# A fused retention and MLP kernel: the first queries and keys split over two DMA queues, and two decays moved from ScalarE to GpSimd

## The chip, the cores and the metric

The kernel runs on one core of one Trainium2 chip. A core has a TensorE (matrix products), a VectorE (DVE in the profile), a ScalarE (ACT), a GpSimd (POOL) and a SyncE (SP, which here only issues transfers). They run side by side and wait for each other through semaphores. SyncE and ScalarE each issue transfers between device memory (DRAM) and on-chip memory (SBUF) on a queue of their own. Matrix products land in PSUM, which TensorE writes and VectorE and ScalarE read.

The metric is device time in microseconds of one execution; lower is better.

## What is computed

First a recurrent retention over 768 tokens, for 4 batches and 8 heads of size 64. Its output, laid out as 3072 tokens of 512 numbers, goes through a two-layer network with a leaky ReLU.

```python
for t in range(S):
    state = gamma[None, :, None, None] * state + np.einsum('bhd,bhe->bhde', k[:, :, t], v[:, :, t])
    y[:, :, t] = scale * np.einsum('bhd,bhde->bhe', q[:, :, t], state)
...
x = np.ascontiguousarray(attn_out.transpose(0, 2, 1, 3)).reshape(B * S, H * D)
h = x @ w_in          # 512 -> 2048
g = np.maximum(0.01 * h, h)
return (g @ w_out)    # 2048 -> 512
```

The weights come as 64-bit floats, and the chip makes 32-bit floats of them.

## The kernel before

**Tiling.** The 768 tokens of a batch are six chunks (c = 0 to 5) of 128. In a chunk the recurrence is written as products: scores of keys and queries, masked (`score`, `masked`), scores times values (`values`), and the state that is carried on (`first_state` for chunk 0). The decay gamma to the power of t is taken out of the products: the values v are multiplied beforehand by a factor for token and head (`decay_v`, L160), and the sums afterwards by another (`tokens_taken`, L300, whose line in the profile is L308). The network is cut into four units of 512 hidden columns; its products are combined in the manner of Strassen, seven for eight.

**Order.** The schedule is by hand: each engine's instructions run in the order of the code, and waits are put in by the framework from what each instruction reads and writes. Chunk 0, batches 0 to 3, is handled as the inputs arrive, and in between the first weight pieces are converted. All the work around the change lies in the first 26 us.

**Steps that the prediction speaks of**, in the order of TensorE:

- `keep_busy(10)` (L897): ten filler products on zeros.
- `score(0, 0)` (L193), on queries and keys of batch 0. `heads[c, b][0]` has shape 128 x 2 x 4 x 128: part 0 of the second axis is the queries, part 1 the keys. The keys are the stationary operand, the queries the moving one.
- three small products (L915 to L919) that spread the table of decays. ScalarE copies the result (L922), and `decay_v` waits for it.
- `score(0, 1)`, then L927, a product that spreads the query factors, which ScalarE copies at L931.
- `values(0, 0)` and `values(0, 1)` (L263 and L252), `score(0, 2)`.
- `direct(0, 0, x, ..., 0)` (L695): the first hidden products, in four steps. Step n needs weight piece n, converted.
- between its steps: `values(0, 2)`, `score(0, 3)`, the states of chunk 0 (L278) and `values(0, 3)`.

**Conversion of a weight piece.** ScalarE makes the powers of two from the top bits (`powers`: L591, L595, L596), VectorE the mantissas (`mantissas_begun`: L603 and L608; `mantissas_ended`: L615, which multiplies the two). L603, L608 and L615 read SBUF only.

**Decays of v.** `decay_v` has two forms. On GpSimd it is one multiplication of 128 x 512 by a broadcast factor (L163). On ScalarE it is eight activations of 128 x 64, one for each head (L167). In chunk 0, batches 0 and 1 take the first form and batches 2 and 3 the second.

**Transfers at the start.** SyncE issues, in this order: queries and keys of batch 0 (`load_qk`, L121), v of batches 0 and 1 (`load_v`, L124), weight pieces 0 and 1 (L542), queries and keys of batch 2, v of batch 2, pieces 2 and 3, queries and keys and v of batch 3, and the keys in their second layout (`load_k`, L127). ScalarE issues queries and keys of batch 1, and the table of decays (L868), which waits for memsets of GpSimd and VectorE (L866, L867). Each transfer counts up one of eight semaphores in turn, so the ninth waits until the first has landed.

Of the kernel before, what the change touches and what calls it, by code (L numbers as in the profile page):

```python
# [22 lines left out]
def kernel(  # L23
# [14 lines left out]
    nc = tc.nc  # L38
# [30 lines left out]
    def unit_tile(k, name):  # L69
        if k in LATE or k in (0, 2):  # L70
            return work.tile([128, 7, 2, 256], FP32, tag=f"late{k}", name=name)
        return const.tile([128, 7, 2, 256], FP32, name=name)
# [32 lines left out]
    heads = {}  # L105
# [14 lines left out]
    def load_qk(c, b, queue=nc.sync):  # L120
        queue.dma_start(out=heads[c, b][0], in_=qk[c, b])  # L121

    def load_v(c, b, queue=nc.sync):
        queue.dma_start(out=heads[c, b][1][:, 1], in_=kv[c, b][:, 1])  # L124
# [30 lines left out]
    def load(c, b, place=None):  # L155
        place_for(c, b, place)
        load_qk(c, b)
        nc.sync.dma_start(out=heads[c, b][1], in_=kv[c, b])

    def decay_v(c, b, engine=nc.gpsimd):  # L160
        v = vals[c, b] if c >= JOINED else heads[c, b][1][:, 1]
        if engine is not nc.scalar:
            engine.tensor_tensor(out=v, in0=v,  # L163
                                 in1=gk[c].unsqueeze(2).to_broadcast([128, H, D]), op=ALU.mult)
        else:
            for h in range(H):
                engine.activation(v[:, h], v[:, h], AF.Identity, scale=gk[c][:, h : h + 1])  # L167
# [43 lines left out]
    def masked(c, b):  # L211
        am = new_am(c, b)
        nc.vector.tensor_tensor(
            out=am.rearrange("p j m n t -> p j m (n t)"),
            in0=scores[c, b].rearrange("p j m n t -> p j m (n t)"),
            in1=mask.rearrange("p n t -> p (n t)").unsqueeze(1).unsqueeze(1)
                .to_broadcast([128, 2, HP // 2, 3 * C // 2]), op=ALU.mult)
        scores[c, b] = am
# [355 lines left out]
    def next_mantissas():  # L574
        begin_mantissas()
        end_mantissas()
# [283 lines left out]
    rows = t[:, 1:3].rearrange("p i k n -> p (i k n)")[:, 0 : decay.shape[1]]  # L860
    nothing = t[:, 0, 0, 0:64].bitcast(BF16)
    half = decay.shape[1] // 2
    load_qk(0, 0)
    load_qk(0, 1, nc.scalar)
    nc.vector.memset(t[:, 0, 0, 0:64], 0.0)
    nc.gpsimd.memset(rows[:, :half], 0.0)  # L866
    nc.vector.memset(rows[:, half:], 0.0)  # L867
    nc.scalar.dma_start(out=rows[0:H], in_=decay)  # L868
    load_v(0, 0)
    load_v(0, 1)  # L870
    load_piece(0)
# [13 lines left out]
    for s in range(2):  # L885
        part = mask[ts(s, 64), 0 : 3 - s : 2 - s]
# [22 lines left out]
    def scratch(name, n):  # L909
# [22 lines left out]
        out=dec[:, 0:n_gq], in_=spread.rearrange("p i n -> p (i n)")))  # L932
# [6 lines left out]
    steps = direct(0, 0, x, parts[0][1], 0)  # L939
    next(steps)  # L940
    next_mantissas()
    decay_v(0, 2, nc.scalar)
    load(1, 2, unit_tile(LATE[0], "in12"))
    masked(0, 2)
    next_powers()
# [4 lines left out]
    score(0, 3)  # L950
    taken(0, 2, x)
    masked(0, 3)
    decay_v(0, 3, nc.scalar)
    next(steps)
    sums0 = two_banks("sums0")
    for b in range(B):
# [532 lines left out]
    for n in range(N2):  # L1489
# [16 lines left out]
        part = gs.pop(n)  # L1506
# [167 lines left out]
```

## Time and profile before

| what | us |
|---|---|
| median of 3 runs (630.54 to 631.47) | 631.17 |
| the profiled execution | 631.22 |
| its span, first to last instruction | 629.3 |

| stretch of the span, us | TensorE busy | VectorE busy | ScalarE busy | GpSimd busy |
|---|---|---|---|---|
| 0 to 13 | 11.55 | 5.69 | 5.27 | 3.33 |
| 13 to 26 | 11.99 | 9.41 | 10.39 | 0.00 |
| 26 to 37 | 10.71 | 8.66 | 10.57 | 0.20 |
| 37 to 629 | 588.58 | 488.61 | 255.16 | 102.24 |

The first table gives the whole time and what the profile covers of it: the span runs from the first to the last instruction, and 1.9 us of the execution lie outside. The second table gives the busy time of four engines in four stretches. A busy time close to the stretch's length means that the engine has hardly a hole there. TensorE's granted clock is 1.00 in all of them.

In the lines of a timeline the first number is the start in us from the begin of the span, the second the duration, then engine, line of the code, operation, what it writes and reads, and at the end, in brackets, how long the engine was idle before it and which work ended that. Names of tiles: `kv` and `in` hold inputs, `ap` the scores, `yp` the sums over values, `d` the hidden products, `w` a weight unit, `raw` a piece of 64-bit weights, `dec` the decay factors.

### The profile page before, as it was taken

Reading aid. Unit: us, or ns where it says so; the run is one execution under the profiler, and the core shown is the slowest. Engines: PE = TensorE matmul, PEld = TensorE weight load, DVE = VectorE, ACT = ScalarE, POOL = GpSimd, SP = SyncE. Lnnn points to the kernel's source line nnn. Section 1 sums busy time; section 2 is a strip of 40 time slices with the busy share of each in tenths; the row PEclk is TensorE's granted clock in tenths of the full one; section 3 lists DMA queues with packets and bytes.
Section 4 is the critical chain, followed back from the end, with each engine's and each line's share of the span. In section 5 each row is a group of like instructions: output and inputs, shape, how many; then the busy total and the mean of one; then the engine's idle time right before and its main releaser. Section 6 shows DMA issues by size and latency. Waiting matters only on the chain.

```text
span 629.3 us, 15220 instructions
## 1 busy us (share of the span) xinstructions
PE 622.8 (99%) x6375; PEld 572.2 (91%) x6375; DVE 512.4 (81%) x793; ACT 281.4 (45%) x543; POOL 105.8 (17%) x109
## 2 busy tenths in 40 slices
PE   8999999999999999999999999999999999999997
PEld 5888888888888889899999999999999999999996
DVE  5679769889979986679888968789968689977796
ACT  5876646446444114352433433534514435534540
POOL 2000000000010110105133052331250321333030
PEclk9999999999999999999999999999999999999999
DMA  8941425547782998396976996988478568678601
GB/s 328 405 143 34 126 75 193 167 133 252 243 296 73 347 333 272 101 339 190 349 228 215 283 333 240 324 280 280 150 257 298 156 216 281 209 264 278 205 1 68
DMA packets 105939, 140.99 MB, mean 224 GB/s; under 512 B 4488, under 2 KB 84232, under 8 KB 105872
## 3 DMA queue, kind: packets, MB, share of 16 engines
q1 hardware_dynamic: 105568, 139.41, 66.6%
q8 instruction: 50, 0.82, 0.5%
q10 hardware_dynamic: 304, 0.62, 0.3%
q14 instruction: 17, 0.14, 0.1%
HBM read 113.54 MB, written 26.48 MB: 222 GB/s over the span
## 4 chain that ended last, share of the span: by engine, by line
PE 94%; DVE 2%; ACT 1%; DMA 1%; issue 0%; SPq 0%; DVEq 0%; ACTq 0%
PE bank L1390 27%; PE bank L1311 12%; PE bank L1351 10%; PE bank L674 9%; PE C_h L674 4%; PE B_o L674 4%; PE A_h L674 4%; PE A_o L674 4%; PE C_o L674 4%; PE B_h L674 4%; PE D_o L674 2%; PE D_h L674 2%; PE d L695 2%; DMA raw<-in_weights_dram 1%; PE bank L371 1%; PE bank L453 1%
## 5 line engine op out<-in xcount | busy, mean ns | idle before, releaser
L619 DVE TENSOR_TENSOR made<-made,bank 128x512 f32<-128x512 f32 (+1 forms) x96 | 55.9, 617 | 39.8 <-PE bank L1390 35.9
L1390 PEld LDWEIGHTS bank<-x,wb 128*128 128x128 f32 x672 | 77.4, 192 | 1.2 <-ACT bank L1394 0.2
L1390 PE MATMUL bank<-x,wb 128*128 128x128 f32 x672 | 78.4, 276 | 0.0
L622 DVE TENSOR_TENSOR g<-g 128x512 f32<-128x512 f32 x96 | 64.0, 688 | 5.2 <-ACT g L1432 0.5
L1390 PE MATMUL bank<-x,wa 128*128 128x128 f32 x512 | 67.7, 275 | 0.0
L1394 ACT COPY bank<-bank 128x512 f32<-128x512 f32 (+1 forms) x32 | 16.6, 517 | 104.6 <-PE bank L1390 97.4
L1390 PEld LDWEIGHTS bank<-x,wa 128*128 128x128 f32 x512 | 62.7, 192 | 0.5 <-ACT made L1400 0.2
L1390 PE MATMUL bank<-t,wa 128*128 128x128 f32 x384 | 53.4, 275 | 0.0
L619 DVE TENSOR_TENSOR g<-made 128x512 f32<-128x512 f32 x64 | 49.0, 786 | 2.9
L1351 PE MATMUL bank<-g,w 128*128 128x256 f32 x216 | 48.5, 381 | 0.0
L1390 PEld LDWEIGHTS bank<-t,wa 128*128 128x128 f32 x384 | 48.0, 192 | 0.0
L1311 PE MATMUL bank<-g,w 128*128 128x128 f32 x368 | 47.0, 276 | 0.0
L1351 PEld LDWEIGHTS bank<-g,w 128*128 128x128 f32 x216 | 40.3, 190 | 5.4
L1311 PEld LDWEIGHTS bank<-g,w 128*128 128x128 f32 x368 | 43.8, 192 | 0.0
L1432 ACT ACTIVATE g<-g 128x512 f32<-128x512 f32 x64 | 37.7, 633 | 6.9 <-DVE g L619 6.9
L1290 POOL TENSOR_TENSOR x<-g 128x512 f32<-128x512 f32 x12 | 16.6, 1382 | 138.2 <-DVE t L622 40.1
L674 PE MATMUL bank<-g,w 128*128 128x256 f32 x168 | 38.0, 382 | 0.0
L674 PEld LDWEIGHTS bank<-g,w 128*128 128x128 f32 x168 | 31.3, 190 | 4.2
L619 DVE TENSOR_TENSOR o<-o,bank 128x512 f32<-128x512 f32 (+2 forms) x44 | 26.5, 633 | 9.8 <-ACT bank L788 4.2
L619 DVE TENSOR_TENSOR o<-o,w 128x2048 f32<-128x2048 f32 (+2 forms) x17 | 28.9, 1722 | 0.2
L674 PE MATMUL A_h<-x,w 128*128 128x256 f32 x112 | 26.6, 380 | 0.0
L163 POOL TENSOR_TENSOR in<-in,dec 128x512 f32<-128x512 f32 x2 | 2.4, 1232 | 139.7 <-DMA in<-in_kv_dram 139.7
(257 smaller groups left out, 1261.1 us busy)
## 6 DMA issues: line engine op xcount, KB each, us to landing
wa<-kept SPq DMA_DIRECT2D x16, 1344.0 KB, 8.7
w<-leaf_kept SPq DMA_DIRECT2D x44, 448.0 KB, 5.4
raw<-in_weights_dram SPq DMA_DIRECT2D x31, 512.0 KB, 4.4
wb<-kept SPq DMA_DIRECT2D x16, 896.0 KB, 6.0
wa<-kept SPq DMA_DIRECT2D x16, 448.0 KB, 4.7
wb<-kept SPq DMA_DIRECT2D x16, 448.0 KB, 6.8
out_dram<-o SPq DMA_DIRECT2D x23, 256.0 KB, 2.9
kept<-w SPq DMA_DIRECT2D x12, 448.0 KB, 5.7
```

Of the source, the lines that this page charges most:

```text
L371: nc.tensor.matmul(at[j][ts(h, 64), n, m, i], lhsT=x[ts(j, 64), 1, a, ts(h, 64)], rhs=x[ts(j, 64), 0, a, ts(h, 64)], start=(n == 0 and a = ...
L453: mm = nc.tensor.matmul(at[n][j][ts(i, 64), m, ts(h, 64)], lhsT=val[ts(h, 64), 2 * a + j], rhs=weights[j][ts(h, 64), n, m, i], start=(n == ...
L619: return nc.vector.tensor_tensor(out=out, in0=a, in1=b, op=ALU.add)
L622: return nc.vector.tensor_tensor(out=out, in0=a, in1=b, op=ALU.subtract)
L674: nc.tensor.matmul(to, lhsT=block(w, sa)[:, k, ts(i, 128)], rhs=rhs[:, k, a:z], start=(first and (i == 0 or split) and n == 0 and k == 0), ...
L695: nc.tensor.matmul(banks[r][:, i, :], lhsT=block(2 * u, r + 2 * kh)[:, k, ts(i, 128)], rhs=x[:, 2 * kh + th, k, :], start=(step == 0 and i ...
L1290: op = nc.gpsimd.tensor_tensor(out=out, in0=a, in1=b, op=ALU.subtract)
L1311: nc.tensor.matmul(ps[q][:, to], lhsT=leaf_weights[i][j], rhs=moving[s][:, i], start=(i == 0 and m in ("M1", "M5", "M4")), stop=True, skip ...
L1351: nc.tensor.matmul(room[x][:, i, :], lhsT=block(2 * u + 1, sa)[:, k, ts(i, 128)], rhs=rhs[:, k, :], start=(first and i == 0 and k == 0), s ...
L1390: nc.tensor.matmul(ps[q][:, i], lhsT=w[:, j, i], rhs=part_of(moving[i], s), start=(i == 0 and m in ("M1", "M5", "M4")), stop=True, skip_gr ...
L1394: nc.scalar.copy(out=ps[3], in_=ps[0])
L1432: nc.scalar.activation(g[:, i], g[:, i], AF.Prelu, alpha=0.01)
```

## The change

The queries and keys of batches 0 and 1 are no longer loaded in one transfer of 512 KB for each batch, but in two of 256 KB. SyncE issues the queries of batch 0 and of batch 1, ScalarE the keys of batch 0, then the table of decays, then the keys of batch 1. The values of batches 2 and 3 of chunk 0 are multiplied on GpSimd (L163, one instruction for each batch) and no longer on ScalarE (L167, eight for each batch). The numbers that are computed are the same.

```diff
-    load_qk(0, 0)
-    load_qk(0, 1, nc.scalar)
+    def load_part(b, part, queue):
+        queue.dma_start(out=heads[0, b][0][:, part], in_=qk[0, b][:, part])
+
+    for b in range(2):
+        load_part(b, 0, nc.sync)
+    load_part(0, 1, nc.scalar)
     nc.vector.memset(t[:, 0, 0, 0:64], 0.0)
     nc.gpsimd.memset(rows[:, :half], 0.0)
     nc.vector.memset(rows[:, half:], 0.0)
     nc.scalar.dma_start(out=rows[0:H], in_=decay)
+    load_part(1, 1, nc.scalar)
     load_v(0, 0)
     load_v(0, 1)
...
-    decay_v(0, 2, nc.scalar)
+    decay_v(0, 2)
...
-    decay_v(0, 3, nc.scalar)
+    decay_v(0, 3)
```

## The prediction

> **What bounds the kernel now.** I read the page first.
>
> ```profile
> PE 622.8 (99%) x6375; PEld 572.2 (91%) x6375; DVE 512.4 (81%) x793; ACT 281.4 (45%) x543; POOL 105.8 (17%) x109
> ```
>
> TensorE is busy 622.8 of 629.3 us. A change at the start can therefore only move the moments at which TensorE works; what it is late by at 26 us it is late by at the end. The second view is the list of TensorE's waits, over the whole span: it shows all that an edit could win there.
>
> ```profile
> PE idle L897 <- DVE t L865: 1.1, 1, 1.1
> PE yp L252 <- issue: 0.7, 1, 0.7
> PE d L695 <- DVE w L615: 0.4, 1, 0.4
> PE ap L193 <- DMA qk<-in_qk_dram: 0.2, 1, 0.2
> PE bank L436 <- DVE made L619: 0.2, 1, 0.2
> ```
>
> The change touches the 0.2 (first scores wait for the first batch's data) and what leads to the 0.4 (first hidden products wait for a converted weight piece). Third, the timeline of TensorE and then of VectorE and GpSimd, from 0 to 20 us (start, duration, engine, line, operation, idle before and what ended it).
>
> ```profile
> 1.05 4.45 PE L897 MATMUL idle<-t 128*128 128x512 bf16 x10 [1.05 <-DVE t L865]
> 5.74 1.20 PE L193 MATMUL ap<-qk 64*64 64x128 f32 x32 [0.24 <-DMA qk<-in_qk_dram]
> 13.38 3.86 PE L695 MATMUL d<-x,w 128*128 128x256 f32 x16 [0.35 <-DVE w L615]
> ```
>
> ```profile
> 9.60 0.92 DVE L603 TENSOR_SCALAR w<-raw 128x512 uint32<-128x512 uint32 x1
> 10.84 0.69 DVE L308 TENSOR_TENSOR x<-yp,dec 128x512 f32<-128x512 f32 x1 [0.33 <-ACT z L595]
> 12.65 0.68 DVE L615 SCALAR_TENSOR_TENSOR w<-w,z 128x512 f32<-128x512 f32 x1
> 13.24 0.42 DVE L603 TENSOR_SCALAR w<-raw 128x512 uint32<-128x512 uint32 x1
> 13.70 0.69 DVE L608 SCALAR_TENSOR_TENSOR w<-raw,w 128x512 f32<-128x512 uint32 x1
> 14.50 0.69 DVE L615 SCALAR_TENSOR_TENSOR w<-w,z 128x512 f32<-128x512 f32 x1
> ```
>
> ```profile
> 8.19 2.04 POOL L163 TENSOR_TENSOR kv<-kv,dec 128x512 f32<-128x512 f32 x2 [5.76 <-ACT dec L922]
> ```
>
> What to see: the ten filler matmuls end at 1.05+4.45 = 5.50, so the scores' wait is 0.24 and no more. From 10.84 to 15.19 VectorE works without a hole: tokens of batches 0 and 1 (L308), then pieces 0 and 1 of the weights (L603, L608, L615). Its L615 of piece 0 ends at 13.33 and releases the first hidden step at 13.38; that of piece 1 ends at 15.19, just when step 0's half of the 3.86 us ends (13.38+1.93 = 15.31). VectorE has no slack there, and TensorE none to give. And L603 took 0.92 while GpSimd's decays ran (to 10.23), 0.42 when they didn't.
>
> Last, the transfers of v of batches 2 and 3, from views of the DMA issues in the windows 5.7 to 6.05 and 7.9 to 8.2 (KB, us to landing): issued at 5.72 and 7.95, they land at 12.3 and 17.9.
>
> ```profile
> in<-in_kv_dram SPq DMA_DIRECT2D x1, 256.0 KB, 6.6
> ```
>
> ```profile
> in<-in_kv_dram SPq DMA_DIRECT2D x1, 256.0 KB, 10.0
> ```
>
> **What the Trainium skill says.** SBUF — State Buffer, Who interferes with whom: a VectorE instruction with two SBUF inputs, or in a two-port mode, and a GpSimd one that reads SBUF exclude each other for the whole instruction; who comes first goes first; a VectorE instruction with one PSUM input is left alone. The trace agrees: the masks L213 (from PSUM) took 0.96 beside GpSimd, as without; at 182 to 185 us, where this same decay meets the same conversion, both engines stretch (timeline of VectorE, then GpSimd):
>
> ```profile
> 182.32 0.69 DVE L615 SCALAR_TENSOR_TENSOR last<-last,z 128x512 f32<-128x512 f32 x1
> 183.93 1.26 DVE L603 TENSOR_SCALAR last<-raw 128x512 uint32<-128x512 uint32 x1 [0.92 <-ACT z L595]
> ```
>
> ```profile
> 182.49 2.42 POOL L163 TENSOR_TENSOR in<-in,dec 128x512 f32<-128x512 f32 x2 [139.72 <-DMA in<-in_kv_dram]
> ```
>
> Two decays alone take 2.04, here 2.42: the first came during L615 and was let through at 183.01, some 0.9 before its end. DMA: Bandwidth & Descriptors, Issuing engines are not separate DMA queues: another issuer saves issue time, not transfer time. The trace agrees in that the two first loads of 512 KB, one on each queue, take 4.9 and 5.1 us to landing.
>
> **The change, part by part.**
>
> Queries and keys. The same 1 MB is cut into four loads of 256 KB. The first half of each of the two 512 KB loads now is all that the first scores need. Both queues move about 0.4 MB per us together (390 to 430 GB/s in most slices of the transfers' view); the whole landed at 5.7 to 5.9, so 512 KB fewer means some 1.3 us less: 4.4 to 4.6, an estimate. That is ahead of 5.50, where the fillers end: the gain is the wait, 0.24, not the 1.3. The keys of batch 1 are issued on ScalarE behind the table of decays (issued at 1.59, held by memsets), near 2.1, and still land about 6, since the bytes are the same; they are needed at 7.5. ScalarE's table load, moved from 2.15 to about 2.6, takes 1.28 and has until 7.6.
>
> SyncE. One more issue ahead of v and piece 0: 0.45. Also, at most eight transfers are in flight: in before the seventh issue of SyncE (ScalarE had two) stands until 5.72, for the first load. With two more loads, piece 1 (2.88 now) becomes the ninth and stands until the first queries have landed, about 4.5. Cost nothing: the queue is full of earlier bytes until piece 0 lands at 9.10. If that cover were gone, piece 1 would cost what it lands after 12.1 instead of 10.4. Rows of 2 KB in place of 4 KB: v's 256 KB take 0.68 us in the stream, half of a 512 KB piece 0.64; over 1 MB that is 0.15. So piece 0 lands at 9.25 to 9.3. ScalarE's L591 and copy L931 then end at 10.5 instead of 10.32, and L308 can start at 10.60 instead of 10.84 (its sums come 0.24 earlier). Slack 0.1; hence the 0.24 arrives whole.
>
> Eight ScalarE activations per batch go (2.00 us each at 13.32 and 19.04). ScalarE is freed, and piece 2 is ready for VectorE 0.5 us earlier (L603 at 16.59 had waited 0.53 for ScalarE). But TensorE runs through from 15.24 to 23.3 with no hole, so this wins nothing.
>
> Two GpSimd multiplies come in, 1.04 us each alone. The first can start when v of batch 2 is there: 12.33+0.12 = 12.45. VectorE by then, 0.24 earlier than now: L615 of piece 0 from 12.41 to 13.09, L603 13.0, L608, L615 of piece 1 to 14.95. All four take two SBUF inputs or the two-port mode. If L615 is first by its 0.04 us, GpSimd holds the ports from 13.09 for 0.9, to 13.99; L603 ends 0.28 after that (as at 10.23 to 10.51), at 14.27 instead of 13.42: +0.85, and L615 of piece 1 ends at 15.80. Step 1 of the hidden products starts at 15.84 instead of 15.24: +0.60. If GpSimd is first, L615 of piece 0 ends near 13.95, step 0 starts at 14.0 (+0.62) and all else moves with it. Both orders give +0.6. Below: if v came after 15 us, or the ports weren't held, -0.24.
>
> The second starts at 18.0, where VectorE does L615 of piece 2 (18.0 to 18.7, moved). TensorE needs that at 19.45 (18.85+0.6). Held back by GpSimd it would end at 19.6: 0 to 0.2 more; I take 0, as the slack is 0.75. L308 and the masks read PSUM and aren't held. The decayed v are needed at 17.8 and 22; GpSimd has them by 14 and 19.1.
>
> Sum: -0.24 + 0.85 = +0.6. From 26 us on the critical chain hangs on TensorE's steps (ScalarE's activations follow them), so it stays. Against the profiled execution, 631.22 (span 629.3 and 1.9 around it): 631.8. It is 0.05 over the median of the runs, so the median too comes to 631.8.
>
> **Rivals.**
>
> Gain only (21%): VectorE makes up for the hold, because GpSimd takes a free place or the ports aren't claimed. For: L603 already stood behind decays at 9.6 without harm. Against: no hole from 10.84 to 15.19. 631.2-0.24 = 630.9; with the 0.66 hole of TensorE at 23.3 (the trace calls it issue; not explained) closed, 630.3.
>
> Slower (19%): the second hold decides too. If VectorE comes to piece 2 more than 0.75 late (point of decision: L615 of piece 2 would end, unhindered, after 19.45), the second hold of 0.9 falls on TensorE as the first did: -0.24+0.85+0.9 = +1.5, 632.7. For: a decay of the pair at 205.5 took 1.49 in such a meeting. Against: the 0.5 us that ScalarE gives back.
>
> No earlier start (7%): the first keys or queries land only near 5.7, since the queues interleave in another way than by halves. Then +0.85: 632.0.
>
> **How the numbers follow.** Forecast 631.8 (53%; its own range 631.3 to 632.4). What a measurement of this kernel can tell from no change is 0.2%, 1.26 us: bounds 629.9 and 632.4. Slower than that: nearly all of the slower rival and a few hundredths of the others: 0.21. Faster: the far end of gain only, 0.04. Range 630.6 to 632.8: it takes in gain only down to part of the closed hole, and the slower rival's middle.
>
> **What would show it.** Scores L193 at 5.50 with no wait for DMA; L163 on GpSimd at about 12.5 or 13.1; one of L615 and L603 there at 1.2 us or more; a hole of 0.6 to 0.9 in TensorE before L695 at 13 to 16 us; no ScalarE L167 at 13 and 19. The prediction is wrong if L163 falls where VectorE reads PSUM or rests, if piece 0 lands after 9.4, or if TensorE's lateness at 26 us isn't what is found at the end.

## The result and the profile after

| kernel | median us | runs | ratio of the runs to before, 95% interval |
|---|---|---|---|
| before | 630.77 | 19 | 1 |
| changed | 632.23 | 19 | 1.0027 (1.0021 to 1.0033) |

The medians differ by 1.46 us; the ratio, which is made from means, says 0.27%, some 1.7 us. It is a slowdown that the measurement can tell. The time lies in the predicted range, 0.43 over the forecast of 631.8, and in part by luck: the forecast was +0.6 on a median of three runs, 631.17, which lies 0.4 above the median of the 19 runs of the kernel before here. The change costs more than twice the +0.6, about what the slower rival said (+1.5), and not for that rival's reason. The profiled execution took 631.97 us with a span of 630.0, only 0.7 more than the span before. That 0.7 looks like the forecast's +0.6 and is not the same thing; the chain of causes is another one, as the timelines show.

TensorE in the changed kernel (line numbers are 5 higher below the edit; start, duration, line, idle before):

```profile
5.43 1.38 PE L193 MATMUL ap<-qk 64*64 64x128 f32 x32
8.06 0.90 PE L193 MATMUL ap<-qk 64*64 64x128 f32 x32 [0.49 <-DMA qk<-in_qk_dram]
12.40 0.90 PE L193 MATMUL ap<-in 64*64 64x128 f32 x32 [0.37 <-DMA in<-in_qk_dram]
13.71 1.99 PE L695 MATMUL d<-x,w 128*128 128x256 f32 x8
16.42 1.99 PE L695 MATMUL d<-x,w 128*128 128x256 f32 x8 [0.71 <-DVE w L615]
20.02 1.99 PE L695 MATMUL d<-x,w 128*128 128x256 f32 x8
```

The first scores start right behind the fillers, 0.31 earlier than before. The second scores, at 7.74 before, now wait for the keys of batch 1 and start at 8.06. Hidden step 0 comes at 13.71 instead of 13.38 (+0.33), step 1 at 16.42 instead of 15.24 (+1.18), step 2 at 20.02 instead of 18.85 (+1.17).

The keys of batch 1, from the view of the DMA issues in the window 2.1 to 2.18 us:

```profile
qk<-in_qk_dram ACTq DMA_DIRECT2D x1, 256.0 KB, 5.8
```

Issued at 2.15, they land 5.8 us later, at 7.93. The same bytes, in the uncut load, had landed at 5.92 before. TensorE had been ready for them since 7.57. VectorE, then GpSimd, in the changed kernel:

```profile
12.97 0.68 DVE L615 SCALAR_TENSOR_TENSOR w<-w,z 128x512 f32<-128x512 f32 x1
13.57 1.27 DVE L603 TENSOR_SCALAR w<-raw 128x512 uint32<-128x512 uint32 x1
18.39 1.34 DVE L615 SCALAR_TENSOR_TENSOR w<-w,z 128x512 f32<-128x512 f32 x1
```

```profile
13.01 1.54 POOL L163 TENSOR_TENSOR in<-in,dec 128x512 f32<-128x512 f32 x1 [3.02 <-DMA in<-in_kv_dram]
18.12 1.08 POOL L163 TENSOR_TENSOR in<-in,dec 128x512 f32<-128x512 f32 x1 [3.56 <-DMA in<-in_kv_dram]
```

The first decay is let through after L615 of piece 0, and L603 of piece 1 stands behind it: 1.27 instead of 0.42, which is the 0.85 of the prediction. The second one holds L615 of piece 2 (1.34 instead of 0.69), and TensorE's step 2 shows no wait.

The list of TensorE's waits tells why the span grew by 0.7 and not by 1.2:

```profile
PE idle L902 <- DVE t L869: 1.1, 1, 1.1
PE d L695 <- DVE w L615: 0.7, 1, 0.7
PE ap L193 <- DMA qk<-in_qk_dram: 0.5, 1, 0.5
PE ap L193 <- DMA in<-in_qk_dram: 0.4, 1, 0.4
PE yp L263 <- issue: 0.2, 1, 0.2
PE bank L436 <- DVE made L619: 0.2, 1, 0.2
```

The 0.7 before L252 ("issue", at 23.3 us) in the first profile of the kernel before is absent. Whether it belongs to the program or to the execution was the first thing to settle.

### The profile page after: what moved, and what is told of

Same layout as the page of the kernel before. It is cut to its first block, busy times and chain, and to the rows that moved or that the text cites. A ratio compares the mean times of both kernels' runs of the same rounds, so it can differ in the third digit from the quotient of the medians.

```text
span 630.0 us, 15213 instructions
## 1 busy us (share of the span) xinstructions
PE 623.0 (99%) x6375; PEld 572.1 (91%) x6375; DVE 512.3 (81%) x793; ACT 277.5 (44%) x527; POOL 108.4 (17%) x111
## 4 chain that ended last, share of the span: by engine, by line
PE 94%; DVE 2%; ACT 1%; DMA 1%; issue 0%; POOL 0%; DVEq 0%; ACTq 0%
PE bank L1395 27%; PE bank L1316 12%; PE bank L1356 10%; PE bank L674 9%; PE C_h L674 4%; PE B_o L674 4%; PE A_h L674 4%; PE C_o L674 4%; PE A_o L674 4%; PE B_h L674 4%; PE D_o L674 2%; PE D_h L674 2%; PE d L695 2%; PE bank L371 1%; PE bank L453 1%; PE bank L382 1%
## 5 line engine op out<-in xcount | busy, mean ns | idle before, releaser
L163 POOL TENSOR_TENSOR in<-in,dec 128x512 f32<-128x512 f32 x4 | 5.2, 1320 | 145.8 <-DMA in<-in_kv_dram 145.8
```

## The experiments

Each variant was timed in 5 to 22 runs beside the kernel before, in three sets, which the third column tells apart. "Half clock" counts the runs whose mean granted clock of TensorE was 0.997 or less. Of the kernel before it was 2 of 51 runs in the first set (630.84), 1 of 29 in the second (630.74) and 10 of 51 in the third (630.92). The ratio is made from means and takes in these runs. The last column is from the one profile of each variant; those of "loads only" and "uncut load behind the table" fell on runs with half clock.

| kernel | median us | before, same set | ratio, 95% interval | half clock | step 0, step 1 (us) |
|---|---|---|---|---|---|
| before, again | 630.91 | 630.84 | 1.0000 (0.9990 to 1.0010) | 2 of 14 | 13.12, 14.98 |
| loads only | 633.33 | 630.84 | 1.0029 (1.0018 to 1.0039) | 12 of 22 | 15.85, 17.71 |
| decays only | 631.86 | 630.84 | 1.0011 (1.0001 to 1.0021) | 1 of 14 | 13.95, 15.81 |
| keys of batch 1 on SyncE | 632.11 | 630.84 | 1.0015 (1.0005 to 1.0025) | 1 of 14 | 13.41, 16.11 |
| cut loads, old queues | 631.61 | 630.74 | 1.0016 (1.0005 to 1.0027) | 0 of 13 | 13.31, 15.17 |
| uncut load behind the table | 633.81 | 630.74 | 1.0047 (1.0035 to 1.0060) | 5 of 5 | 16.19, 18.05 |
| loads only, keys ahead of the table | 631.18 | 630.74 | 1.0005 (0.9997 to 1.0013) | 1 of 13 | 13.42, 15.26 |
| loads only, hole filled | 632.41 | 630.74 | 1.0022 (1.0012 to 1.0032) | 0 of 9 | 14.62, 16.48 |
| first decay only | 631.55 | 630.92 | 1.0009 (1.0000 to 1.0018) | 4 of 22 | 14.16, 16.02 |
| second decay only | 631.26 | 630.92 | 0.9998 (0.9987 to 1.0009) | 1 of 14 | 13.68, 15.54 |
| changed, keys ahead of the table | 631.92 | 630.92 | 1.0010 (1.0002 to 1.0019) | 0 of 14 | 13.20, 15.90 |
| one queue, eight fillers | 630.71 | 630.92 | 0.9998 (0.9985 to 1.0011) | 2 of 14 | 12.89, 14.75 |

**Is the hole at 23.3 us the program's? The kernel before, again.** No edit.

> The kernel before, unchanged, for a second profile. TensorE's starts up to 23 us should come out within 0.1 us of the first profile. The hole of 0.66 us before L252 at 23.3: if it is tied to the program it is there again; if it is chance it may be missing, the span is then 0.66 shorter, and the first pair of profiles understates the change's cost by that much.

The whole list of TensorE's waits in this second profile:

```profile
PE idle L897 <- DVE t L865: 1.1, 1, 1.1
PE yp L263 <- ACT z L596: 0.4, 1, 0.4
PE d L695 <- DVE w L615: 0.3, 1, 0.3
PE bank L436 <- DVE made L619: 0.2, 1, 0.2
```

No hole at 23.3: the same program runs with it and without it, and against this profile the changed kernel is 1.6 us late when the hidden products of the second token half begin (26.83 against 25.27), no longer 0.6. TensorE's starts differ by up to 0.27 between the two profiles (the load of batch 0 landed at 5.50 here and at 5.70 there), so 0.1 was too tight an expectation.

**The two parts alone.** Loads only leaves the decays on ScalarE:

```diff
-    decay_v(0, 2)
+    decay_v(0, 2, nc.scalar)
...
-    decay_v(0, 3)
+    decay_v(0, 3, nc.scalar)
```

> Only the loads of the change; the decays of batches 2 and 3 stay on ScalarE. Theory 1, two delays that add (late keys of batch 1, then the port hold): the keys of batch 1 land near 7.9 us, the second scores start near 8.0 instead of 7.74, hidden step 0 at 13.7 (before 13.38), step 1 at 15.55 (before 15.24), no L603 or L615 over 0.75 us; time 0.3 us over before. Theory 2, the hold alone costs: step 0 at 13.4 or earlier, time as before. Theory 3, rows of 2 KB make piece 0 late and that costs: L308 of batch 0 waits for ScalarE's copy, not for the sums of TensorE; 0.3 over before too.

Decays only has the loads of before and both decays on GpSimd.

> Only the decays on GpSimd; the loads as before. Theory 1: v of batch 2 lands at 12.3, the decay starts at 12.4 and holds L615 of piece 0 (planned for 12.65) to about 13.95, so hidden step 0 starts near 14.0 (before 13.38) and step 1 near 15.95 (before 15.24); time 0.6 to 0.9 over before. Theory 3 (transfers alone cost): steps at 13.4 and 15.25, time as before.

The decays alone behave as foretold, here with GpSimd first (GpSimd, then VectorE):

```profile
12.31 1.04 POOL L163 TENSOR_TENSOR in<-in,dec 128x512 f32<-128x512 f32 x1 [2.05 <-DMA in<-in_kv_dram]
```

```profile
12.67 1.22 DVE L615 SCALAR_TENSOR_TENSOR w<-w,z 128x512 f32<-128x512 f32 x1
13.82 0.41 DVE L603 TENSOR_SCALAR w<-raw 128x512 uint32<-128x512 uint32 x1
```

L615 is held, L603 isn't; step 0 comes at 13.95, +0.57. The loads alone, which I had booked as a gain, cost more than the decays, and much more than the 0.3 us of theory 1. The times fall into two groups: 10 runs from 631.1 to 632.2, with a median of 631.5, 0.7 over before, and 12 from 633.3 to 635.0, those with half clock. The profile of the loads alone fell into the second group (TensorE):

```profile
8.66 1.56 PE L193 MATMUL ap<-qk 64*64 64x128 f32 x32 [1.68 <-DMA qk<-in_qk_dram]
10.15 2.01 PE L932 MATMUL spread<-t 128*128 128x512 f32 x2
```

In the changed kernel's profile, at full clock, the same two groups took 0.90 and 1.12 us. The view of windows has, in each line, the stretch and its length, busy us of TensorE, its weight loads, VectorE, ScalarE and GpSimd, then the granted clock, the DMA share and GB/s:

```profile
1.70:5.10 3.40, 3.40 (x9) 1.06 (x7) 0.01 (x1) 1.28 (x1) 0.58 (x2) 1.00 0.90 267
5.10:8.50 3.40, 1.88 (x39) 1.49 (x38) 0.96 (x1) 0.20 (x1) 1.04 (x1) 1.00 1.00 342
8.50:12.00 3.50, 3.34 (x34) 1.89 (x34) 1.29 (x2) 0.67 (x1) 1.04 (x1) 0.51 1.03 412
12.00:15.40 3.40, 3.28 (x98) 2.59 (x97) 2.09 (x4) 3.10 (x6) 0.00 (x0) 1.00 1.02 407
```

In 5.1 to 8.5 TensorE works 1.88 of 3.4 us, since the second scores wait until 8.66; in the next stretch its clock is halved. The clock record of the trace has the half clock for 3.41 us, so the loss is at most about 1.7; the two groups above are 1.55 us longer. The Trainium skill, TensorE: Matmul & The Clock Gate, section What's actually happening, describes a window of 3.4 us and half the clock after an idle one. The length agrees; the window here was not idle but a little over half busy, and the half clock came all the same.

**Is the half clock the hole's doing?** Loads only, with four fillers in the hole:

```diff
+    keep_busy(4)
     score(0, 1)
```

> The loads of the change, all decays of v as before, and four filler products more in TensorE's hole before the second scores (they change no result). Theory C, a hole of TensorE above about 1.5 us in the first 9 us is answered with half the clock in the next stretch of 3.4 us, which is what sets the slower half of the runs of the loads alone: runs with clock 0.997 or less go away, and the median falls from 633.3 to 631.3 to 632.0. Rival: the slower half is late data; then the spread of 631 to 635 stays.

Half clock is gone in all 9 runs (12 of 22 without the fillers), although the data still come late, so the hole is what calls it. In this profile TensorE worked 2.66 of the 3.4 us from 5.3 on and kept its full clock. The median of 632.41 is 0.4 over what I expected: here the keys landed at 8.85, still 1.0 us after the fillers, and step 0 came at 14.62. The fillers cure the clock, not the late data.

**Why are the keys late?** Two theories: short rows and more transfers, or the place in ScalarE's queue. Cut loads, old queues:

```diff
-    load_qk(0, 0)
-    load_qk(0, 1, nc.scalar)
+    for b in range(2):
+        for part in range(2):
+            (nc.sync, nc.scalar)[b].dma_start(out=heads[0, b][0][:, part], in_=qk[0, b][:, part])
```

> Loads only: each first load cut into queries and keys, but batch 0 stays on SyncE and batch 1 on ScalarE, ahead of the table of decays; all decays of v as before. Theory A, short rows or the number of transfers make one of the sixteen parts of each transfer late: piece 0's last part lands 0.4 us or more behind its median part, as in the changed kernel, and the time is 0.5 or more over before. Theory B, the late issue of the keys of batch 1 behind the table is what costs: they land by 6.0, the second scores start without a wait near 7.6, the time is within 0.3 of before.

The last part of piece 0 lands 0.29 behind its median, not 0.4, and the second scores start at 7.67 with no wait. That much fits the queue theory. The median, 0.9 over before, is more than it allows; two of the 13 runs (634.07 and 634.31, at full clock) stand apart, and I can't explain them. What short rows cost by themselves stays open: 0.9 here, 0.4 in the repaired loads below.

Uncut load behind the table, all else as before:

```diff
-    load_qk(0, 1, nc.scalar)
...
     nc.scalar.dma_start(out=rows[0:H], in_=decay)
+    load_qk(0, 1, nc.scalar)
```

> The kernel before, but the uncut load of batch 1 goes behind the table of decays on ScalarE's queue; all decays of v as before. Theory B: it lands near 8 us, TensorE stands 0.5 us or more before the second scores, and in a part of the runs the granted clock is 0.997 or less; time 0.5 to 2 over before. Theory A: rows are 4 KB, nothing is late but for the 0.5 us of issue; time within 0.4 of before.

This decides that the place matters: with rows of 4 KB and no cut, the place behind the table alone makes the data late (issued at 2.23, DMA issues in the window 2.2 to 2.3):

```profile
qk<-in_qk_dram ACTq DMA_DIRECT2D x1, 512.0 KB, 6.7
```

TensorE then stands 1.9 us, and all five runs, of the same set as the filled hole, have half clock (TensorE's timeline, then the windows):

```profile
9.00 1.56 PE L193 MATMUL ap<-qk 64*64 64x128 f32 x32 [1.90 <-DMA qk<-in_qk_dram]
```

```profile
5.50:8.90 3.40, 1.60 (x38) 1.43 (x38) 0.96 (x1) 0.20 (x1) 1.42 (x2) 1.00 0.98 390
8.90:12.30 3.40, 3.30 (x34) 1.86 (x34) 1.29 (x2) 0.68 (x1) 0.62 (x1) 0.50 1.04 411
```

The packets of ScalarE's queue say where the time goes. Here the table is the first transfer on that queue. It is issued at 1.59, its first packet moves at 4.26 and its last ends at 4.89; the load behind it, issued at 2.23, moves its first packet at 5.19. In the changed kernel the keys of batch 0 have the queue until 4.18, the table's packets run from 4.48 to 4.78, and the keys of batch 1 begin at 5.48, 3.3 us after their issue and 1.3 us after the keys of batch 0 were through. SyncE's first load, for comparison, was issued at 0.80 and moved its first packet at 1.83. So a transfer of 8 rows and 30 KB took 2.7 us to start and held what stood behind it, while SyncE's queue moved on: in the changed kernel v of batch 0 landed at 6.22, before at 7.08. Why the table starts so late isn't shown: no run separates its few rows from its later issue or from the bytes that SyncE had issued ahead of it.

**The repair, in three forms.** Keys of batch 1 ahead of the table, without and with the decays on GpSimd:

```diff
     load_part(0, 1, nc.scalar)
+    load_part(1, 1, nc.scalar)
...
     nc.scalar.dma_start(out=rows[0:H], in_=decay)
-    load_part(1, 1, nc.scalar)
```

> The loads of the change, but on ScalarE's queue both keys ahead of the table; all decays of v as before. Theory B: keys of batch 1 land by 6.0, no wait before the second scores, hidden step 0 at 13.1 to 13.4, clock 0.999 or 1.000 in nearly all runs; time from 0.3 under to 0.2 over before. Theory A: the keys may come in time, but piece 0 lands at 9.5 or later in its last part, and the time is 0.5 or more over.

> The whole changed kernel, but on ScalarE's queue both keys ahead of the table of decays. If the queue behind the table is the larger part of the change's cost: no wait before the second scores, clock 0.999 or 1.000 in nearly all runs, and the time falls from 1.7 over before to 0.6 to 1.0 over, what the port hold costs. If not, it stays at 1.4 or more.

Or on SyncE, behind the two queries:

> The whole change, but the keys of batch 1 issued by SyncE right behind the two queries. Theory 1: they land near 6, the second scores start at 7.5 without a wait, step 0 at 13.1 to 13.2; the hold of the first decay stays (one of L615, L603 at 1.2 us or more), step 1 at 15.8 to 15.9; time 0.5 to 0.6 over before and 0.6 under the changed kernel. Theory 3: piece 0 lands as late as in the changed kernel and step 0 stays at 13.6 to 13.7.

Loads only, repaired, is within measurement of before (1.0005), and 2.2 us under the unrepaired loads; most of that is half clock, as the unrepaired runs at full clock have 631.5. In the changed kernel the repair takes the ratio from 1.0027 to 1.0010. Of the runs at full clock alone the medians are 632.2 without and 631.9 with it, so the place in the queue is worth some 0.3 us there. The rest lies in the half clock: 4 of 19 runs without the repair, none of 14 with it, but 10 of 51 of the kernel before in the repair's own set. These counts don't show that the repair removes it. What is left by the medians, 1.0 us, is as much as the decays alone cost (631.86 against 630.84). On SyncE it helps less: the second scores don't wait (7.48), but the queries and keys of batch 2 land at 12.2, and the third scores stand 0.9 us. That wait is also in the repaired loads (TensorE's timeline):

```profile
7.51 0.90 PE L193 MATMUL ap<-qk 64*64 64x128 f32 x32
12.36 0.90 PE L193 MATMUL ap<-in 64*64 64x128 f32 x32 [0.88 <-DMA in<-in_qk_dram]
```

It shows what the half MB that came earlier is worth: TensorE reaches the third scores earlier and stands there, because the bytes of batch 2 come no sooner. In this profile the last of the sixteen parts of piece 0 landed at 9.63, 0.67 behind the median part, as in the changed kernel (9.68, 0.93 behind). In the cut loads on the old queues it was 0.29. The keys of batch 1 have such late parts too. In the changed kernel their median part landed at 7.11, in time for TensorE at 7.57, and only the last, at 7.93, made it wait; in the other two profiles with these loads the median parts came at 7.28 and 7.00 and the last at 8.53 and 8.85. Ahead of the table (loads only) the median part came at 5.71, the last at 6.21. So the place in the queue moves the whole load, by some 1.4 us, and a late part adds up to 1.9. I have no cause for these late parts.

**Which decay costs?** Only `decay_v(0, 2)`, and only `decay_v(0, 3)`, on GpSimd, with the loads of before.

> Of the change only the decay of batch 2 on GpSimd; loads and batch 3 as before. Port theory: L615 of piece 0 or L603 of piece 1 takes 1.2 us or more, hidden step 0 near 13.95 and step 1 near 15.8 as with both decays moved; time 0.5 to 0.9 over before, all of the cost of both. Rival, the two decays share the cost: half of that.

> Of the change only the decay of batch 3 on GpSimd; loads and batch 2 as before. Port theory: it meets VectorE's conversion of piece 2 at 18 us; before, that one ends at 18.53 and step 2 starts at 18.85, so a hold of 0.6 moves step 2 by 0.2 to 0.4 here (no first hold gives slack); steps 0 and 1 as before; time 0 to 0.4 over. Rival: no cost at all, step 2 at 18.6 to 18.9.

The first alone shows the hold, L615 of piece 0 at 1.35 us and step 0 at 14.16 after a wait of 1.02; its ratio of 1.0009 is nearly that of both (1.0011). The second alone is the instructive one (VectorE, then TensorE):

```profile
16.90 0.43 DVE L603 TENSOR_SCALAR w<-raw 128x512 uint32<-128x512 uint32 x1 [0.55 <-ACT z L595]
18.16 1.51 DVE L615 SCALAR_TENSOR_TENSOR w<-w,z 128x512 f32<-128x512 f32 x1
```

```profile
19.72 1.99 PE L695 MATMUL d<-x,w 128*128 128x256 f32 x8 [0.51 <-DVE w L615]
```

Here ScalarE still does batch 2, VectorE waits 0.55 for it, and the second hold does reach TensorE: step 2 waits 0.51. In the changed kernel the same hold costs nothing, because the first one has already made TensorE late. The ratio doesn't resolve this half microsecond (0.9987 to 1.0009); the medians of the runs at full clock, 631.25 against 630.78, agree with it.

**A version that beats both?** Uncut loads of both batches on SyncE, so that the table has ScalarE's queue for itself, eight fillers for ten, and the copy of the query factors ahead of the powers of piece 0:

```diff
-    load_qk(0, 1, nc.scalar)
+    load_qk(0, 1)
...
-    keep_busy(10)
+    keep_busy(8)
...
-    next_powers(scratch("m5", 0), lambda: nc.scalar.copy(
-        out=dec[:, 0:n_gq], in_=spread.rearrange("p i n -> p (i n)")))
+    nc.scalar.copy(out=dec[:, 0:n_gq], in_=spread.rearrange("p i n -> p (i n)"))
+    next_powers(scratch("m5", 0))
```

> The kernel before with three edits: the uncut loads of batches 0 and 1 both on SyncE, so that the table is alone on ScalarE's queue; eight fillers for ten; the copy of the query factors ahead of the powers of piece 0. Theory: queries and keys of batch 0 land near 4.6, those of batch 1 by 6.0, the table by 5.8; scores start near 4.7, L308 of batch 0 near 9.7, and hidden step 0 waits only for the scores of batch 2 (their data land at 11.7): 12.9 against 13.1 to 13.4. Time 0.2 to 0.5 under before. Rival: TensorE's holes before 9 us now reach the clock, and some runs are 1.7 longer.

```profile
4.58 1.56 PE L193 MATMUL ap<-qk 64*64 64x128 f32 x32
11.68 0.90 PE L193 MATMUL ap<-in 64*64 64x128 f32 x32 [0.46 <-DVE w L608]
12.89 3.42 PE L695 MATMUL d<-x,w 128*128 128x256 f32 x14
```

The steps come where they were expected, 12.89 for step 0, but the scores that start 1.2 us sooner are paid for by a wait at the third ones. The time, 630.71 against 630.92, can't be told from before. It is clearly under the changed kernel, but no better than the old one.

## Why the prediction was right and wrong

**The start of the scores: right.** At 5.43 without a wait for data; the gain of 0.24 was 0.31, and 0.11 against the second profile of before. The scores themselves took 1.38 us instead of 1.20, since TensorE is not yet at its full clock there: the clock record has it from 6.50 on (6.43 before), and the first ten fillers took 0.44 us each, the four in the filled hole, later, 0.26. The 1.00 that the view of windows prints for stretches before that doesn't tell this.

**The keys of batch 1: the step that failed.** The prediction said that they "still land about 6, since the bytes are the same; they are needed at 7.5". They landed at 7.93. Equal bytes did not give an equal landing, because one of the two queues stood still: ScalarE's moved nothing from 4.18 to 5.48 us but the table's 30 KB, and the keys stood behind the table. The prediction had the issue times of that queue (1.59 and 2.1) and took issue for start. That the place behind the table makes a load late is shown by the uncut load, which is late in the same way, and by the repair; why the table is slow to start, and why the last part of the keys came 0.8 us after the median one, stays open. In the sum the term of -0.24 should have been +0.33, the amount by which step 0 is late in this profile.

**The gain of 0.24 would not have come whole in any case.** With the keys ahead of the table, step 0 came at 13.42 (decays on ScalarE) and 13.20 (on GpSimd), against 13.38 and 13.12 in the two profiles of before. The third scores stood 0.88 and 0.58 us there for the queries and keys of batch 2, which landed at 12.23 and 11.96 and not, as before, at 11.67. The prediction asked only when piece 0 lands and gave the data of batch 2 no term.

**What that step can trigger: not foreseen.** In the loads alone a hole of 1.7 us was followed by 3.4 us of half clock, and fillers in the hole removed it. Of the changed kernel 4 of 19 runs have half clock (median 633.8, the other 15: 632.2). Whether the hole calls it there too isn't shown: the one profile has a hole of 0.5 us and full clock, and the kernel before, whose two profiles have no such hole, has it in 13 of 131 runs. No rival had it. The rival "no earlier start" asked the right question of the wrong load: the first keys came in time, the second didn't.

**Piece 0 at 9.25 to 9.3: too early.** It landed at 9.68. The slack of 0.1 would not have borne that, had the sums over values not been late themselves: L308 of batch 0 waited for TensorE, until 11.16.

**The port hold: right in place and size.** +0.85 at L603 and a hole of 0.71 before step 1 (0.6 to 0.9 expected). Both engines came 0.56 us later than foretold, GpSimd at 13.01 and not 12.45, L615 at 12.97 and not 12.41, so that L615 was first by the same 0.04. That is chance, but little hangs on it: with GpSimd first (decays only, first decay only) L615 was 0.54 and 0.67 longer, and step 0 waited 1.02 in both, for 0.35 before. By the medians at full clock the hold is +0.7 (first decay) to +1.0 (both).

**The second hold: right for this kernel.** L615 of piece 2 ended at 19.73, and step 2 began at 20.02, right behind the scores, without a wait. The slower rival named slack as the point of decision, and the second decay alone shows it on the other side of that point.

**ScalarE's relief wins nothing: right.** ScalarE began on piece 2 at 14.83, earlier than at 15.23, and step 2 is as late as step 1.

**The sum.** At step 1, +1.18 was measured where +0.6 was forecast: 0.57 from the keys, the rest as said. The first pair of profiles hides this behind a hole that comes and goes (0.66 at 23.3 us). The prediction noted the hole as unexplained but carried TensorE's lateness over it as if it were fixed. With the second profile of before the spans differ by 1.0 and the starts at 26 us by 1.6, near the 1.4 by which the medians at full clock differ (632.2 against 630.8). The rest of the mean ratio are the runs with half clock.

## What to carry to other kernels

Count for each queue what stands ahead of a load, and from which moment it moves; equal bytes aren't enough. Here a transfer of 30 KB kept the keys behind it back by more than a microsecond, and putting it behind them removed their wait. Before moving work to GpSimd, list which VectorE instructions at that moment work in SBUF alone: here each meeting made L603 or L615 longer by 0.5 to 0.9 us, and the whole time only where the chain had no slack. Look at runs with half clock and runs without it separately; the kernel before has some too. One profile of each kernel isn't enough for differences under a microsecond: a second profile of the same kernel shows which holes belong to the program.

## What the runs showed that was not expected

- A transfer of 8 rows (30 KB), first on its queue, moved its first packet 2.67 us after its issue, against about 1.0 for the first load of 128 rows on SyncE's queue; the load behind it began 0.3 to 0.7 us after the small one's last packet (two profiles). The cause is open.
- TensorE's clock was halved for 3.41 us after stretches of 3.4 us in which it had worked 1.60 and 1.88 us (ends of products are modelled); after one with 2.66 us it wasn't.
- A hole of 0.66 us in TensorE at 23.3, with no releaser in the trace, was there in one of two profiles of the same program. The three repaired variants show one of 0.36 to 0.56 us in the same group of products (`values(0, 3)`). The cause is open.
